# Attention and a mixture of experts on one core: zero stores put in another order around the weights, one weight load issued earlier in the queues, the last scaling split over two engines

## The chip, the core and the metric

The kernel runs on one core of a Trainium2 chip. The core has a matrix engine (TensorE, PE in the profile, with its weight loads as PEld), a vector engine (VectorE, DVE), a scalar engine (ScalarE, ACT), a general engine (GpSimd, POOL) and a queue engine (SyncE, SP) that issues transfers. Sixteen transfer engines move data between the core's memory and HBM. The metric is the device time of one execution in microseconds; lower is better.

## The reference, cut to what matters

The first part is attention inside chunks of 64 positions, for 8 batches, 8 heads and 576 positions of 64 numbers. Its output, seen as 4608 tokens of 512 numbers, goes into a layer of 8 experts. Each token goes to the expert with the largest logit; of these an expert keeps at most 80, those with the largest gate. All other rows of the output are zero.

```
logits = x @ w_gate
expert_idx = np.argmax(logits, axis=1)
...
out = np.zeros((N, D), dtype=np.float32)
for e in range(E):
    ...
    if len(tok_idx) > capacity:
        gw = gate_w[tok_idx]
        keep = np.argpartition(-gw, capacity)[:capacity]
        tok_idx = tok_idx[keep]
    h = np.maximum(x[tok_idx] @ w1[e], 0.0)
    out[tok_idx] = gate_w[tok_idx, None] * (h @ w2[e])
```

Each expert has 2 MiB of first-layer weights (512 x 1024, float32) and 2 MiB of second-layer weights (1024 x 512). The output has 9 MiB.

## The kernel before, in words

Three stages follow each other. In the first, to about 127 us, the attention is computed and its result x stored in HBM (`xs`), and the gates are counted on the way. In the second, to about 142 us, the kept tokens of each expert are found and numbered; TensorE runs matmuls without use (`keep_warm`) between the short steps. The third stage is the experts'.

There the kept tokens stand in 768 slots, 96 to an expert, in six rounds of 128 slots (r = 0 to 5), four groups of 32 slots each, so that a round takes in two or three experts. Rounds 0 and 1 use experts 0 to 2, round 2 experts 2 and 3, round 3 experts 4 and 5, round 4 experts 5 and 6, round 5 experts 6 and 7. `experts` writes out the order of one round:

- `gather(r)`: an indirect load from `xs` on POOL's queue. Rounds 0 to 2 are gathered whole (tile `xg`) at the start of the stage, rounds 3 to 5 in four quarters each (`quarters`, tile `xq`), paced by a copy of one column on POOL.
- `xpose(r)`: transposes on TensorE and copies on ScalarE (`xt`).
- `layer1(r, 0)` and `layer1(r, 1)`: the first layer for two groups each, L237; ReLU on ScalarE (`hs`), a transpose on VectorE (`ht`).
- `layer2(r)`, called one round later: the second layer, L254, its sum `y` scaled by the gates on VectorE into `ys` (L259).
- `scatter(r)`: an indirect store of the 128 scaled rows into `out` on POOL's queue. The scatters of rounds 0, 1 and 2 are written out together after round 3, the others one by one.

All weights and all zero stores go through SP's queue, in the order in which they are written out. The weights are issued a part at a time by `part(e, l)`: expert e, layer l (0 or 1); w1_3 below is part(3, 0), the fourth expert's first-layer weights, and w2_6 is part(6, 1). Experts 0 and 1 are loaded during the attention, experts 2, 3, 4 and 7 share three buffers, and 5 and 6 take those of 0 and 1. `clear(n)` stores zeros over 512 rows of `out` (1 MiB), `clear(3.5, nc.sync, 2)` over 256. A scatter waits until all of them have landed.

A part can be held back: `part(..., after)` first copies one column of `after` into the new tile, and the load has to wait for that copy. Before, w1_3 is held back by `si`, the scatters' row numbers, which VectorE ends with. `ahead(r, xg)` is called as `extra` after the first gathers and after each round: with r = 0 it issues w1_4 and w2_3, held back until the second gather has landed; r = 1 issues w1_5, w2_4 and the zero stores `CLEARS[1]`; r = 2 issues w1_6, w2_5 and `CLEARS[2]`; r = 3 issues w1_7 and w2_6; r = 4 issues w2_7.

So SP's queue before, from 122 us on, holds: w2_2, zeros 0, zeros 2, w1_3, zeros 3.5, w1_4, w2_3, w1_5, w2_4, zeros 1, 4, 5, w1_6, w2_5, zeros 6, 7, 8, w1_7, w2_6, w2_7.

A block for the general case stands behind the experts (L1179); its condition is false with these inputs.

Of the kernel before, what the change touches and what calls it, by code (L numbers as in the profile page):

```python
# [11 lines left out]
AF = mybir.ActivationFunctionType  # L12
ALU = mybir.AluOpType
# [13 lines left out]
DM = 512  # L27
FF = 1024
SL = 96
NR = NE * SL // P  # L30
# [3 lines left out]
NWARM = 17  # L34
WARM = (2, 3, 5)
BIG = 8192.0
CLEARS = {1: (1, 4, 5), 2: (6, 7, 8)}
NQ = 3
ON_POOL = (0, 1)
STEPS_AFTER = 6  # L40
# [29 lines left out]
def attention_moe(ctx: ExitStack, tc: tile.TileContext, qk0, qv, kh, wg, w1, w2, cap, cst, out):  # L70
    nc = tc.nc
# [22 lines left out]
    scale = cp.tile([40, NE], F32, name="scale")  # L94
# [94 lines left out]
    def experts(pool, pp, gi, si, gate, getw, tag, extra=None, quarter=None):  # L189
        groups = [[(4 * r + g) // 3 for g in range(4)] for r in range(NR)]  # L190
        xg, xT, hT, hs, ys_ = {}, {}, {}, {}, {}

        def gather(r):
            t = pool.tile([P, DM], F32, name=f"xg{tag}{r}", tag="xg", bufs=NQ if extra else 2)
            nc.gpsimd.indirect_dma_start(
                out=t, out_offset=None, in_=xs[:, :],
                in_offset=bass.IndirectOffsetOnAxis(ap=gi(r), axis=0),
                bounds_check=NT * 512 - 1, oob_is_err=False)
            xg[r] = t

        def xpose(r):
            t = pool.tile([P, 4, P], F32, name=f"xt{tag}{r}", tag="xt")
            n = 4 if r else 2
            for b0 in range(0, 4, n):
                pm = pp.tile([P, n, P], F32, name=f"xp{tag}{r}_{b0}", tag="hp" if b0 else "xp",
                             bufs=2 if b0 else 1)
                for b in range(n):
                    nc.tensor.transpose(
                        pm[:, b, :], xg[r].rearrange("p (m b) -> p b m", b=4)[:, b0 + b], ident)
                nc.scalar.copy(t[:, b0:b0 + n], pm)  # L210
            xT[r] = t.rearrange("p b (g t) -> p g b t", g=4)

        def quarters(r, after):
            pace = pool.tile([P, 1], F32, name=f"pace{tag}{r}", tag="pace", bufs=1)
            nc.gpsimd.tensor_copy(pace, after)
            t = pool.tile([P, DM], F32, name=f"xq{tag}{r}", tag="xg", bufs=NQ)
            for g in range(4):
                nc.gpsimd.indirect_dma_start(
                    out=t[:, P * g:P * g + P], out_offset=None,
                    in_=xs.rearrange("r (c d) -> (r c) d", c=4),  # L220
                    in_offset=bass.IndirectOffsetOnAxis(ap=quarter(4 * r + g), axis=0),
                    bounds_check=NT * 2048 - 1, oob_is_err=False)
            xg[r] = t

        def xpose_blocks(r):
            t = pool.tile([P, 4, 4, 32], F32, name=f"xt{tag}{r}", tag="xt")
            nc.vector.transpose(t, xg[r].rearrange("p (g t b) -> p g b t", g=4, b=4))
            xT[r] = t

        def layer1(r, f):  # L230
            h = pp.tile([P, 2, 256], F32, name=f"h{tag}{r}_{f}", tag="h", bufs=4)
            for j in range(2):
                g = 2 * f + j
                w = getw(groups[r][g])[0]
                for b in range(4):
                    for c in range(4):
                        nc.tensor.matmul(  # L237
                            h[32 * c:32 * c + 32, j, :], lhsT=xT[r][:, g, b, :],
                            rhs=w[:, b, 256 * c:256 * c + 256],
                            start=(b == 0), stop=(b == 3), tile_position=(0, 32 * c))  # L240
            a = pool.tile([P, 512], F32, name=f"hs{tag}{r}_{f}", tag="hs", bufs=1)
            nc.scalar.activation(a, h.rearrange("p j n -> p (j n)"), AF.Relu)  # L242
            t = pool.tile([P, 2, 8, 32], F32, name=f"ht{tag}{r}_{f}", tag=f"ht{f}")
            nc.vector.transpose(t.rearrange("p j b n -> p (j b n)"), a)  # L244
            hs[r] = a[:, 0:1]
            hT[r, f] = t

        def layer2(r):
            y = (pp.tile([P, DM], F32, name=f"y{tag}{r}", tag="h", bufs=4) if extra and r == NR - 1
                 else pp.tile([P, DM], F32, name=f"y{tag}{r}", tag="y", bufs=1))  # L250
            for c in range(8):
                for g in range(4):
                    o = 32 * g
                    nc.tensor.matmul(  # L254
                        y[o:o + 32, :], lhsT=hT[r, g // 2][:, g % 2, c, :],
                        rhs=getw(groups[r][g])[1][:, c, :],
                        start=(c == 0), stop=(c == 7), tile_position=(0, o))
            ys = pool.tile([P, DM], F32, name=f"ys{tag}{r}", tag="ys", bufs=3 if extra else 1)
            nc.vector.tensor_scalar(ys, y, gate[:, r:r + 1], None, op0=ALU.mult)  # L259
            ys_[r] = ys  # L260

        def scatter(r):
            nc.gpsimd.indirect_dma_start(  # L263
                out=out, out_offset=bass.IndirectOffsetOnAxis(ap=si[:, r:r + 1], axis=0),
                in_=ys_.pop(r), in_offset=None, bounds_check=NT * 512 - 1, oob_is_err=False)

        for r in range(NQ if extra else 2):
            gather(r)
        if extra:
            extra(0, xg)  # L270
        xpose(0)
        for r in range(NR + 1):
            if r < NR:
                layer1(r, 0)
            if r + 1 < (NQ if extra else NR):
                xpose(r + 1)
            if r < NR:
                layer1(r, 1)
            if extra and NQ <= r + 1 < NR:
                xpose_blocks(r + 1)  # L280
            if extra and NQ <= r + 2 < NR:
                quarters(r + 2, hs[r])
            if not extra and r + 2 < NR:
                gather(r + 2)
            if r >= 1:
                layer2(r - 1)
            if extra:
                extra(r + 1, xg)
            while ys_ and (r >= NQ or not extra):
                scatter(min(ys_))  # L290


    with ExitStack() as actx:
# [539 lines left out]
        def clear(n, eng=nc.scalar, m=4):  # L833

            r0 = int(512 * n)
            eng.dma_start(
                out[r0:r0 + P * m].rearrange("(p c b) d -> p c (b d)", p=P, b=2),
                zero[:, None, :].to_broadcast([P, m // 2, 2 * DM]))
# [38 lines left out]
        with tc.manual_schedule():  # L877
# [234 lines left out]
            gate, sv = targets(mp, [(pl0, gi0), (pl1, gi1)], "c")  # L1112
# [19 lines left out]
            si = mp.tile([P, NR], I32, name="si")  # L1132
# [11 lines left out]
    with tc.manual_schedule():  # L1144
        with ExitStack() as ectx:
            ep = ectx.enter_context(tc.tile_pool(name="exp", bufs=2, reuse_waits="tile"))
            pp = ectx.enter_context(tc.tile_pool(name="pexp", bufs=2, space=PSUM,
                                                 reuse_waits="tile"))

            def part(e, l, after=None):  # L1150

                w = weights.setdefault(e, [None, None])
                pool = wp if e in (5, 6) else wp2
                a, n = ((4, FF), (8, DM))[l]
                w[l] = pool.tile([P, a, n], F32, name=f"w{l + 1}_{e}", tag=f"w{l + 1}")
                if after is not None:
                    nc.vector.tensor_copy(w[l][:, 0, 0:1], after)
                fetch(w[l], e, l, 0, a)

            def ahead(r, xg):  # L1160

                if r < 5:
                    for e, l in (((4, 0), (3, 1)), ((5, 0), (4, 1)),
                                 ((6, 0), (5, 1)), ((7, 0), (6, 1)), ((7, 1),))[r]:
                        part(e, l, xg[1][:, 0:1] if r == 0 else None)
                for n in CLEARS.get(r, ()):
                    clear(n, nc.sync)

            part(2, 0)
            part(2, 1)  # L1170
            clear(0, nc.sync)
            clear(2, nc.sync)
            part(3, 0, si[:, 0:1])
            clear(3.5, nc.sync, 2)
            experts(ep, pp, lambda r: gi1[:, r - 1:r] if r else gi0, si, gate, weights.get, "c",
                    ahead, lambda g: giq[:, g % 4, g // 4 - NQ:g // 4 - NQ + 1])


    with tc.If(nc.values_load(flag_i[0:1, 0:1], min_val=0, max_val=1) > 0):  # L1179
        with ExitStack() as gctx:  # L1180
# [9 lines left out]
            with ExitStack() as lctx:  # L1190
                lp = lctx.enter_context(tc.tile_pool(name="gpl", bufs=1, space=PSUM))
                with tc.For_i(0, 28, 1):
# [10 lines left out]
                        th, pc, capt, th, op0=ALU.is_ge, op1=ALU.mult)  # L1203
# [36 lines left out]
            with tc.For_i(0, nc.values_load(nr[0:1, 0:1], min_val=0, max_val=48), 1):  # L1240
                with ExitStack() as lctx:
                    xp = lctx.enter_context(tc.tile_pool(name="gx", bufs=1))
                    si = xp.tile([P, NR], I32, name="gsi")
                    with ExitStack() as pctx:
# [4 lines left out]
                        gate, sv = targets(xp, [pl], "g")  # L1249
# [90 lines left out]
```

## Time and profile before

| | us |
|---|---|
| median of three runs | 240.34 |
| the three runs | 239.62, 240.34, 243.28 |
| profiled execution | 239.95 |
| its span, first to last instruction | 238.2 |
| TensorE busy | 220.3 |
| VectorE busy | 130.5 |
| ScalarE busy | 73.7 |
| POOL busy | 64.2 |

The profile is of one execution. A row of the timeline gives the start in us from the span's beginning, the length, the engine, the line, the operation and its tiles (written<-read, buffer numbers left out, a tile's name often with a `c` at its end), and in brackets the idle time before it and what ended that. A row of an operation's table gives the shortest, median and longest time in ns, and the first and last start. A row by stretch has for each engine its busy time and, in parentheses, its number of instructions (PE, PEld, DVE, ACT, POOL), then TensorE's granted clock as a share of the full one, the share of time in which the transfer engines were busy, and what they moved in GB/s. "SPq" and "POOLq" are what the queues of these engines do themselves, such as issuing a transfer.

### The profile page before, as it was taken

The page shows a single profiled execution, that of the slowest core. Times are in us where ns is not written, and L with a number is a line of the kernel's source. Part 1 is how long each engine was busy: PE and PEld are TensorE (multiplying, and loading weights), DVE is VectorE, ACT ScalarE, POOL GpSimd, SP SyncE. Part 2 cuts the span into 40 slices and gives each one's busy share as a digit, 9 for nine tenths or more (in the row PEclk, how much of TensorE's full clock was granted, in tenths as well). Part 3 has the DMA queues.
Part 4 walks back from the last instruction along what each step waited for, and adds up shares of the span by engine and source line. Part 5 has one row for each costly group of instructions (what it writes and reads, how often), then busy time and mean ns, then how long its engine had stood idle before and what let it go on. Part 6 is the DMA issues. An engine that isn't in the chain of part 4 may idle for free. (4 is left out here: it accounts for less than half of the span.)

```text
span 238.2 us, 8194 instructions
## 1 busy us (share of the span) xinstructions
PE 220.3 (92%) x3513; PEld 140.8 (59%) x3513; DVE 130.5 (55%) x411; ACT 73.7 (31%) x161; POOL 64.2 (27%) x145
## 2 busy tenths in 40 slices
PE   7998999998998999999998999999999999999910
PEld 5787787876787787878764635643535344453300
DVE  6587697878689898969877771121122214020110
ACT  3124434342645445666764411210101101020000
POOL 9001221121203047473534050015070420111130
PEclk9999999999999999999999999999999999999995
DMA  6999999999999999999999939999999999994120
GB/s 214 358 408 389 408 415 407 416 410 417 410 415 409 389 413 382 405 349 388 375 406 416 416 128 316 376 415 400 398 417 414 411 412 418 411 412 158 66 76 1
DMA packets 24121, 84.81 MB, mean 356 GB/s; under 512 B 2768, under 2 KB 2896, under 8 KB 24080
## 3 DMA queue, kind: packets, MB, share of 16 engines
q1 hardware_dynamic: 20272, 71.84, 76.4%
q0 software_dynamic: 3664, 12.32, 13.4%
q8 instruction: 30, 0.49, 0.8%
q10 hardware_dynamic: 144, 0.07, 0.2%
q14 instruction: 11, 0.09, 0.1%
HBM read 64.03 MB, written 20.45 MB: 355 GB/s over the span
## 5 line engine op out<-in xcount | busy, mean ns | idle before, releaser
L237 PE MATMUL hc<-w,xtc 128*32 128x256 f32 x768 | 42.8, 379 | 0.2 <-ACT xtc L210 0.2
L254 PE MATMUL yc<-w,htc 128*32 128x512 f32 x384 | 42.1, 592 | 0.0
L401 PE MATMUL s<-kz,qv 128*64 128x128 f32 x544 | 37.2, 279 | 0.0
L237 PEld LDWEIGHTS hc<-w,xtc 128*32 128x32 f32 x768 | 24.7, 110 | 18.3 <-issue 2.4
L437 ACT ACTIVATE pT<-pt 128x512 f32<-128x512 f32 x36 | 21.4, 594 | 37.0 <-PE pt L435 36.9
L401 PEld LDWEIGHTS s<-kz,qv 128*64 128x64 f32 x544 | 29.0, 136 | 5.7 <-issue 5.6
L417 DVE TENSOR_REDUCE mx<-s 128x8 f32<-128x512 f32 (+1 forms) x37 | 24.9, 674 | 12.6 <-PE s L401 12.3
L254 PEld LDWEIGHTS yc<-w,htc 128*32 128x32 f32 x384 | 12.5, 110 | 26.6 <-issue 25.7
L460 PEld LDWEIGHTS o<-qv,pT 64*64 64x64 f32 x1120 | 19.9, 134 | 12.0 <-issue 8.2
L242 ACT ACTIVATE hsc<-hc 128x512 f32<-128x512 f32 x12 | 7.2, 597 | 62.7 <-PE hc L237 62.7
L244 DVE STREAM_TRANSPOSE htc<-hsc 128x512 f32<-128x512 f32 x12 | 8.5, 710 | 32.9 <-ACT hsc L242 32.9
L460 PE MATMUL o<-qv,pT 64*64 64x65 f32 x1120 | 25.0, 224 | 1.1 <-issue 0.8
L419 DVE TENSOR_TENSOR sm<-s,mx 128x512 f32<-128x512 f32 (+1 forms) x37 | 24.7, 667 | 0.1
L479 DVE TENSOR_TENSOR x<-o,rc 128x512 f32<-128x512 f32 x35 | 24.1, 689 | 0.8
L435 PE MATMUL pt<-ct,sm 128*128 128x128 f32 x144 | 23.9, 289 | 0.0
L259 DVE TENSOR_SCALAR ysc<-yc,gatec 128x512 f32<-128x512 f32 x6 | 4.5, 751 | 34.3 <-PE yc L254 26.2
L497 PE MATMUL px<-ct,x 128*128 128x128 f32 x136 | 20.5, 273 | 0.0
L498 ACT COPY xT<-px 128x512 f32<-128x512 f32 x32 | 18.6, 580 | 0.0
L575 POOL TENSOR_TENSOR comp<-comp,ct 128x32 bf16<-128x32 bf16 x18 | 3.9, 237 | 50.2 <-DVE rc L474 40.6
L435 PEld LDWEIGHTS pt<-ct,sm 128*128 128x128 f32 x144 | 15.6, 143 | 2.4
L497 PEld LDWEIGHTS px<-ct,x 128*128 128x128 f32 x136 | 15.9, 140 | 0.8 <-issue 0.8
L263 POOL DMA_INDIRECT out<-ysc,si x6 | 6.0, 994 | 32.6 <-issue 12.6
(205 smaller groups left out, 231.5 us busy)
## 6 DMA issues: line engine op xcount, KB each, us to landing
w<-in_w SPq DMA_DIRECT2D x12, 2048.0 KB, 21.6
qv<-in_qv SPq DMA_DIRECT2D x14, 1032.0 KB, 11.4
kz<-in_kh SPq DMA_DIRECT2D x34, 256.0 KB, 10.4
xs<-x POOLq DMA_DIRECT2D x8, 1024.0 KB, 10.5
w<-in_w SPq DMA_DIRECT2D x8, 1024.0 KB, 11.2
out<-zero SPq DMA_DIRECT2D x8, 1024.0 KB, 19.4
qv<-in_qv SPq DMA_DIRECT2D x2, 520.0 KB, 8.9
qv<-in_qv SPq DMA_DIRECT2D x2, 516.0 KB, 9.4
```

The source lines that it names most:

```text
L237: nc.tensor.matmul(h[32 * c:32 * c + 32, j, :], lhsT=xT[r][:, g, b, :], rhs=w[:, b, 256 * c:256 * c + 256], start=(b == 0), stop=(b == 3), ...
L244: nc.vector.transpose(t.rearrange("p j b n -> p (j b n)"), a)
L254: nc.tensor.matmul(y[o:o + 32, :], lhsT=hT[r, g // 2][:, g % 2, c, :], rhs=getw(groups[r][g])[1][:, c, :], start=(c == 0), stop=(c == 7), ...
L401: nc.tensor.matmul(o, lhsT=a, rhs=b, start=True, stop=True)
L417: nc.vector.tensor_reduce(m8, s8, axis=AX.X, op=ALU.max)
L419: d['sub'] = lambda: nc.vector.tensor_tensor(d8, s8, to, op=ALU.subtract)
L435: nc.tensor.transpose(pt[:, pr, :], sv[:, pr, :], ident)
L437: nc.scalar.activation(pT, pt, AF.Exp, scale=0.125)
L460: nc.tensor.matmul(po[h][64 * u:64 * u + 64, 65 * pr:65 * pr + 65], lhsT=d['pT'][64 * h:64 * h + 64, pr, 64 * u:64 * u + 64], rhs=TT[T, r] ...
L479: nc.vector.tensor_tensor(x8, pov[..., 0:64], to, op=ALU.mult)
L497: nc.tensor.transpose(pm[:, pr, :], t['x'][:, r, P * pr:P * pr + P], ident)
L498: copy(t['xT'][:, :, P * r:P * r + P], pm)
```

## The change

Three things change.

1. The zero stores' order. Zeros 2 no longer stand ahead of the experts; they are stored in `CLEARS[2]`, and zeros 6 move from there into `CLEARS[1]`.
2. w1_3 and the half store behind it (zeros 3.5) are issued from a call of `ahead` with r = -1 that stands between the second and the third gather. What holds w1_3 back is now a copy of a gate column on POOL's queue, which stands behind the second gather's issue, in place of the copy of `si` on VectorE.
3. The last round's scaling is done in two halves of 256 columns, the first on VectorE, the second on ScalarE as a copy with a scale.

SP's queue then holds: w2_2, zeros 0, w1_3, zeros 3.5, w1_4, w2_3, w1_5, w2_4, zeros 1, 4, 5, 6, w1_6, w2_5, zeros 2, 7, 8, w1_7, w2_6, w2_7.

```
-CLEARS = {1: (1, 4, 5), 2: (6, 7, 8)}
+CLEARS = {1: (1, 4, 5, 6), 2: (2, 7, 8)}
...
-            nc.vector.tensor_scalar(ys, y, gate[:, r:r + 1], None, op0=ALU.mult)
+            h = DM // 2 if extra and r == NR - 1 else DM
+            nc.vector.tensor_scalar(ys[:, 0:h], y[:, 0:h], gate[:, r:r + 1], None, op0=ALU.mult)
+            if h < DM:
+                nc.scalar.activation(ys[:, h:], y[:, h:], AF.Copy, scale=gate[:, r:r + 1])
             ys_[r] = ys
...
         for r in range(NQ if extra else 2):
             gather(r)
+            if extra and r == 1:
+                extra(-1, gate)
         if extra:
             extra(0, xg)
...
-            def part(e, l, after=None):
+            def part(e, l, after=None, eng=nc.vector):
...
                 if after is not None:
-                    nc.vector.tensor_copy(w[l][:, 0, 0:1], after)
+                    eng.tensor_copy(w[l][:, 0, 0:1], after)
                 fetch(w[l], e, l, 0, a)
 
             def ahead(r, xg):
 
+                if r < 0:
+                    part(3, 0, xg[:, 0:1], nc.gpsimd)
+                    clear(3.5, nc.sync, 2)
+                    return
...
             clear(0, nc.sync)
-            clear(2, nc.sync)
-            part(3, 0, si[:, 0:1])
-            clear(3.5, nc.sync, 2)
             experts(ep, pp, lambda r: gi1[:, r - 1:r] if r else gi0, si, gate, weights.get, "c",
                     ahead, lambda g: giq[:, g % 4, g // 4 - NQ:g // 4 - NQ + 1])
```

## The prediction

> **What bounds the kernel now.** I read the page's two top sections, then the chain that ended last, then the timeline of the expert part from 137 us on, and last single landings of transfers.
>
> ```profile
> PE 220.3 (92%) x3513; PEld 140.8 (59%) x3513; DVE 130.5 (55%) x411; ACT 73.7 (31%) x161; POOL 64.2 (27%) x145
> ...
> 226.43 0.98 DMA out<-ysc,si
> ...
> 230.19 0.69 POOL out L263
> ```
>
> TensorE is busy nearly all the time, but the chain at the end is not its own: it goes from scatter to scatter on the POOL queue. The timeline of the end shows why.
>
> ```profile
> 203.01 1.02 POOL L263 DMA_INDIRECT out<-ysc,si  x1 [10.66 <-SPq L1179]
> 206.30 7.09 PE L237 MATMUL hc<-w,xtc 128*32 128x256 f32 x128
> 210.88 1.01 POOL L263 DMA_INDIRECT out<-ysc,si  x1 [6.85 <-DMA out<-ysc,si]
> 213.21 13.92 PE L254 MATMUL yc<-w,htc 128*32 128x512 f32 x128
> 218.55 0.98 POOL L263 DMA_INDIRECT out<-ysc,si  x1 [6.66 <-issue]
> 221.98 0.98 POOL L263 DMA_INDIRECT out<-ysc,si  x1 [2.45 <-DVE ysc L259]
> 226.43 0.98 POOL L263 DMA_INDIRECT out<-ysc,si  x1 [3.47 <-issue]
> 227.19 0.75 DVE L259 TENSOR_SCALAR ysc<-yc,gatec 128x512 f32<-128x512 f32 x1 [6.12 <-PE yc L254]
> 229.90 0.98 POOL L263 DMA_INDIRECT out<-ysc,si  x1 [2.49 <-issue]
> ```
>
> The six scatters write one tensor and go one at a time. Scatter 4 leaves at 226.43 although its matmuls (the first half of the 13.92 us) ended near 220.2; scatter 5 leaves at 229.90 although its scaling ended at 227.94. What starts this chain is the last zero store. The next fence has, for single transfers, the issuing instruction (its start is the last time but one in the row) and under it the time to landing: the last zero store (rows 4096 to 4607) and scatter 0. The two rows at its end are SP's notices of landed weights: that of w1_7 (first layer of expert 7), and six whose first is w2_6 and whose last is w2_7 (second layers).
>
> ```profile
> L836 SPq DMA_DIRECT2D out<-zero x1: 2448/2448/2448, 182.7 to 182.7; - x1
> DMA to landing us min/median/max: 19.4/19.4/19.4
> ...
> L263 POOL DMA_INDIRECT out<-ysc,si x1: 1025/1025/1025, 203.0 to 203.0; - x1
> DMA to landing us min/median/max: 7.0/7.0/7.0
> ...
> L1179 SPq EVENT_SEMAPHORE  x1: 17/17/17, 207.1 to 207.1; - x1
> ...
> L1179 SPq EVENT_SEMAPHORE  x6: 17/17/17, 212.5 to 218.4; - x6
> ```
>
> The last zeros land at 182.7 + 19.4 = 202.1, scatter 0 leaves 0.9 us later, lands at 210.0 behind the weights; scatter 2 follows scatter 1 as late (7.7 us), and from 218.55 on the spacings are 3.43, 4.45 and 3.47 us. The weights are close behind too: w2_6 lands at 212.5 and is wanted at 213.2 by the second layer, w1_7 lands at 207.1 and is wanted by the second group of layer 1, a quarter of 7.09 us after 206.30, at 208.1. w2_7 lands by 218.4 and is wanted at 220.2. So three streams end almost together: TensorE with 0.7 to 2 us to spare, the weights, and the scatters, which are last.
>
> All of it hangs on one transfer queue. The page's row of 40 slices has its engines at nine tenths or more but for the first slice, one at 137 to 143 us and those from 214 on:
>
> ```profile
> DMA  6999999999999999999999939999999999994120
> ...
> 138.00:139.00 1.00, 1.00 (x17) 0.27 (x15) 1.00 (x10) 0.00 (x0) 0.36 (x1) 1.00 0.08 33
> 140.00:141.00 1.00, 1.00 (x8) 0.39 (x6) 0.90 (x7) 0.00 (x0) 0.95 (x1) 1.00 0.15 57
> 155.00:160.00 5.00, 5.00 (x84) 2.48 (x77) 1.14 (x2) 0.93 (x2) 0.36 (x2) 1.00 1.04 421
> 165.00:170.00 5.00, 5.00 (x100) 3.03 (x96) 1.39 (x2) 0.60 (x1) 0.00 (x0) 1.00 1.03 393
> ```
>
> In the rows by stretch the last two columns are the share and the rate (GB/s) of the transfer engines. Soon after 137 us they have little to do.
>
> **The change, part by part.** Times here are against the profiled execution (239.95 us, span 238.2), which lies 0.4 us under the median of the three runs.
>
> *The zero stores.* Store 2 and its landing, as above for single transfers:
>
> ```profile
> L836 SPq DMA_DIRECT2D out<-zero x1: 641/641/641, 123.7 to 123.7; - x1
> DMA to landing us min/median/max: 17.3/17.3/17.3
> ```
>
> Before, stores 0 and 2 (1 MiB each) go out one behind the other from 123 us on, the second landing at 123.7 + 17.3 = 141.0, and fill most of the queue until about 137. After, store 2 leaves that place and goes into the later round; store 6 moves up a round, ahead of w1_6 and w2_5. So the full queue gets 1 MiB more, all of it ahead of the last zero store and of w1_7, w2_6 and w2_7, and the idle stretch grows by as much. At 421 and 393 GB/s 1.049 MB take 2.49 and 2.67 us: I take 2.55 (some 411 GB/s). The Trainium skill ("DMA: Bandwidth & Descriptors", Specifications) gives about 358 GB/s as the limit of memory traffic for one core. By it the store would cost an estimated 2.9 us and the sum below would be some +2.3; the rows, at 393 and 421, stand against it.
>
> What the removal frees is the first gather.
>
> ```profile
> 137.21 1.15 POOL L195 DMA_INDIRECT xgc<-xs,gic  x1 [2.93 <-DVE bt L1077]
> 139.94 1.00 POOL L195 DMA_INDIRECT xgc<-xs,gic  x1 [1.58 <-DVE rowc L182]
> 140.32 1.10 PE L828 MATMUL pwarm<-ct 128*128 128x512 f32 x2
> 141.25 1.00 POOL L195 DMA_INDIRECT xgc<-xs,gic  x1 [0.30 <-issue]
> 141.66 0.75 PE L208 MATMUL xpc<-ct,xgc 128*128 128x128 f32 x4 [0.24 <-DMA xgc<-xs,gic]
> 141.88 0.15 DVE L1157 CAST w<-si 128x1 f32<-128x1 int32 x1
> 142.06 0.38 SPq L113 DMA_DIRECT2D w<-in_w  x1
> 144.16 0.15 DVE L1157 COPY w<-xgc 128x1 f32<-128x1 f32 x1 [1.94 <-DMA xgc<-xs,gic]
> ...
> 153.95 0.75 PE L208 MATMUL xpc<-ct,xgc 128*128 128x128 f32 x4
> ...
> 172.87 0.18 POOL L215 COPY pacec<-hsc 128x1 f32<-128x1 f32 x1 [8.11 <-ACT hsc L242]
> 173.67 1.02 POOL L218 DMA_INDIRECT xqc<-xs,giq  x1 [0.62 <-DVE htc L244]
> ```
>
> Its transposes wait 0.24 us for it, since the warm-keeping matmuls hold TensorE until 141.42. However early it lands, the experts begin at most 0.24 us sooner, and that only lengthens the wait for weights: nothing at the end.
>
> *w1_3 behind the second gather.* The pacing copy moves from VectorE (141.88) to POOL, between gather 1 (ends 140.94) and gather 2. Like the copy at 172.87 it takes 0.18, and the next gather follows 0.62 later, so gather 2 leaves some 0.7 us later, near 142.0. Gather 1 took 4.2 us from its start to 144.16; gather 2, beside the weights, may take more, but its transposes stand at 153.95 (the last xpc row): free. The copy starts between 140.95 and 141.25, as gather 2 did; its source, the gates, is long done. SP can issue w1_3 between 141.2 and 141.5 instead of 142.06, 0.6 us earlier, and the half store behind it as well. That is the gain: the stream starts 0.6 us sooner (bounds 0.3, should POOL take the copy up late, and 0.85). SP then waits for gather 1 as before (144.16): 2.5 MiB are queued, over 6 us of work, so the queue does not run dry even if gather 1, now beside w1_3, lands 1 us later. VectorE is rid of 0.15 us that nobody waits for.
>
> *The last scaling in halves.*
>
> ```profile
> L259 DVE TENSOR_SCALAR ysc<-yc,gatec 128x512 f32<-128x512 f32 x6 | 4.5, 751 | 34.3 <-PE yc L254 26.2 <-DMA out<-ysc,si 8.1
> L210 ACT COPY xtc<-xpc 128x256 f32<-128x256 f32 x2 | 0.6, 375 | 2.3 <-PE xpc L208 2.3
> ```
>
> 751 becomes about 400 ns, with ScalarE's half beside it at 375: 0.35 us earlier, at most 0.38, at worst 0 (if ScalarE is as slow as VectorE's whole). It is hidden behind scatter 4's landing, by 229.90 - 227.94 = 2.0 us. Without that cover it would be worth its 0.35.
>
> *The sum.* Stream: +2.55 - 0.6 = +1.95 (bounds +1.6 and +2.4). Then w1_7 lands at 209.05, where the second group of layer 1 could go on at 207.85: a stall of 1.2 us; w2_6 at 214.45 against 214.15, 0.3 more; w2_7 at 220.35 is wanted only at 221.4. TensorE ends at 214.45 + 13.92 = 228.4, against 227.13. The last zeros land at 204.05; scatter 0 leaves near 204.95, lands near 212.0, and as the weights behind it are as many as before, the whole chain keeps its distances: scatter 5 leaves at 231.85, with y scaled at 228.8. The end of the kernel follows scatter 5 as now. So +1.95 us: 241.9 from the profiled execution, 242.3 from the median. I say 242.0: the profiled execution lies between the two lower of the three runs (239.62 and 240.34), and stands for a usual one.
>
> The chain has a play of its own: from scatter 3 to 4 it took 4.45 us where its neighbours took 3.43 and 3.47. I leave that as it is, but 1 us may go, or come at another scatter. With the stream's bounds that makes +0.6 to +3.4, or 240.6 to 243.4.
>
> **Rivals.** *Not slower: the queue's slowest engine decides, and it loses nothing.* After 138 us the transfer rate is down to 33 and 57 GB/s: a few of the 16 engines lag. Store 2 lands only at 141.0, against w1_3's issue at 142.06. If the engine that lags sets the later landings too and its lag lasts into w1_3, it never pauses: its transfers are as many as before in either order, store 2's place costs it nothing, and what is left is the 0.6 us of w1_3: scatter 5 at 229.3, 239.4 us. It decides once the lag reaches past w1_3's issue, 1.1 us more than it does. Against it: 141.0 lies before 142.06, so the lag is gone when the stream starts. 0.16.
>
> *Slower, by a second long landing.* ScalarE's last instructions, now over long before, move behind its half of the scaling, beside scatter 5. If that, or the shifted weights, gives two more spacings of 4.45 instead of 3.45 us, the chain has +1.95 + 2 = 243.9. For it: of the three late spacings one is that long. Against: no weights are in flight there. 0.11.
>
> *A long hold-up, and the clock with it.*
>
> ```profile
> 227.00:228.00 1.00, 0.12 (x4) 0.00 (x0) 0.75 (x1) 0.00 (x0) 0.41 (x1) 1.00 0.05 20
> ...
> 232.00:233.00 1.00, 0.00 (x0) 0.00 (x0) 0.00 (x0) 0.00 (x0) 0.00 (x0) 0.54 0.07 29
> ```
>
> The second row is the first stretch of 1 us in which the granted clock (0.54) is not full, some 5 us after the last matmul (0.12 us into the row of 227); the expected stall is 1.2. So the clock needs a stall four times as long, such as POOL's copy would make if it were held up: 3.5 us there bring the stream, and with it the end, 3.5 us later still, to 245.4, even at full clock. 0.04.
>
> *It does not do what it says*: w1_3 may go no earlier, if POOL's copy starts after gather 2's old time. That is +2.55, inside the forecast's bounds.
>
> **Chances and range.** Forecast 0.69, not slower 0.16, long landings 0.11, stall or hold-up 0.04. The range takes the forecast's bounds and reaches to the not-slower case's 239.4 and the long landings' 243.9. Two per cent (4.8 us) is about what a measurement of this kernel can tell from no change: faster than 235.5 no case gives (0.02 for what I overlooked), slower than 245.1 the last one, 0.05; within, 0.93.
>
> **What would show it.** Right: w1_3 issued near 141.4; the transfer queue idle from about 134.5; the last zero store landing near 204; PE waiting for a weight transfer at L237 and L254 near 208 and 214; scatters 0 and 5 near 205 and 231.9; scatter 5 still released by scatter 4 and not by the scaling. Wrong: zeros landing at 202 or before, no wait for weights, or scatter 5 released by the halves. The prediction fails as a whole if the stream is not full, so that 1 MiB more finds room.

## The result and the profile after

The changed kernel takes 242.44 us (median of 22 runs, 240.31 to 244.5), the kernel before 239.44 (22 runs, 238.62 to 243.28). The ratio, from undisturbed runs, is 1.0104, 95% interval 1.0079 to 1.0129: slower by 1.0%, some 2.5 us (3.0 by the two medians). The forecast was +2.0 us, 242.0 in all.

The profile shown is of an execution of 240.31 us, the quickest of the 22, so the 2.5 us are not all in it. Its span is 238.2 us, as before. First its page's rows by 40 slices (transfer share and rate), then the stretches of 1 us with engines, clock, share and rate:

```profile
DMA  6999999999999999999999649999999999996220
GB/s 220 354 406 389 410 415 407 415 413 416 410 415 411 390 407 396 404 338 396 379 406 414 266 107 334 409 411 398 402 418 414 411 407 411 413 415 259 74 73 8
...
134.00:135.00 1.00, 0.95 (x12) 0.64 (x11) 0.18 (x1) 0.17 (x1) 0.05 (x1) 1.00 0.61 246
...
137.00:138.00 1.00, 1.00 (x4) 0.44 (x3) 1.00 (x8) 0.00 (x0) 1.00 (x1) 1.00 0.00 0
```

The queue empties in the slice from 131 us on (266 GB/s) and moves nothing from 137 to 138. Before, it was full until 137:

```profile
134.00:137.00 3.00, 2.94 (x28) 2.13 (x27) 1.63 (x11) 0.22 (x2) 0.19 (x1) 1.00 1.01 414
```

The idle stretch has grown by the 1 MiB taken out of it. The start of the experts, from the timeline of the changed kernel:

```profile
136.99 1.15 POOL L195 DMA_INDIRECT xgc<-xs,gic  x1 [2.93 <-DVE bt L1082]
139.72 1.01 POOL L195 DMA_INDIRECT xgc<-xs,gic  x1 [1.58 <-DVE rowc L182]
140.72 0.21 POOL L1162 COPY w<-gatec 128x1 f32<-128x1 f32 x1
140.95 0.37 SPq L113 DMA_DIRECT2D w<-in_w  x1
141.03 0.64 PE L208 MATMUL xpc<-ct,xgc 128*128 128x128 f32 x4
141.08 1.02 POOL L195 DMA_INDIRECT xgc<-xs,gic  x1 [0.16 <-issue]
```

POOL's copy stands right behind the second gather and w1_3 leaves at 140.95, 3.96 us after the first gather where it was 4.85: 0.89 us sooner. This execution reached the experts 0.22 us earlier than that of before, so distances from the first gather say more than the times themselves.

The end: SP's notices of landed transfers, then the timeline.

```profile
L1185 SPq EVENT_SEMAPHORE  x2: 17/17/17, 201.9 to 203.4; - x2
L1185 SPq EVENT_SEMAPHORE  x1: 17/17/17, 208.5 to 208.5; - x1
L1185 SPq EVENT_SEMAPHORE  x6: 17/17/17, 214.3 to 220.7; - x6
...
204.33 1.02 POOL L266 DMA_INDIRECT out<-ysc,si  x1 [12.73 <-SPq L1185]
208.53 5.39 PE L237 MATMUL hc<-w,xtc 128*32 128x256 f32 x96 [1.07 <-SPq L1185]
213.74 14.50 PE L254 MATMUL yc<-w,htc 128*32 128x512 f32 x128
222.87 0.98 POOL L266 DMA_INDIRECT out<-ysc,si  x1 [2.44 <-DVE ysc L260]
226.76 0.98 POOL L266 DMA_INDIRECT out<-ysc,si  x1 [2.91 <-issue]
228.28 0.48 DVE L260 TENSOR_SCALAR ysc<-yc,gatec 128x256 f32<-128x256 f32 x1 [6.12 <-PE yc L254]
228.80 0.47 ACT L262 ACTIVATE ysc<-yc,gatec 128x256 f32<-128x256 f32 x1 [14.22 <-DVE ysc L260]
230.25 0.98 POOL L266 DMA_INDIRECT out<-ysc,si  x1 [2.51 <-ACTq L1185]
```

The last zeros land at 203.4 (202.1 before), w1_7 at 208.5 (207.1), w2_6 at 214.3 (212.5). TensorE, which did not wait for weights before, stands still for 1.07 us ahead of 208.53. The bracket names SP's own notice, as that comes at the moment w1_7 lands. The last row of L254 is 14.50 us long instead of 13.92, and w2_6, which its third group needs at once, lands 0.6 us after the row's start. Scatter 0 leaves 67.34 us after the first gather (65.80 before), scatter 5 93.26 (92.69).

### The profile page after: what moved, and what is told of

Its sections match the earlier page's. It is cut to its first block, busy times and chain, and to the rows that moved or that the text cites. A ratio compares the mean times of both kernels' runs of the same rounds, so it can differ in the third digit from the quotient of the medians.

```text
span 238.2 us, 8197 instructions
## 1 busy us (share of the span) xinstructions
PE 218.9 (92%) x3513; PEld 142.3 (60%) x3513; DVE 130.0 (55%) x410; ACT 74.2 (31%) x162; POOL 64.8 (27%) x146
## 5 line engine op out<-in xcount | busy, mean ns | idle before, releaser
L254 PE MATMUL yc<-w,htc 128*32 128x512 f32 x384 | 42.7, 592 | 0.0
L254 PEld LDWEIGHTS yc<-w,htc 128*32 128x32 f32 x384 | 15.7, 110 | 24.0 <-issue 17.1
L260 DVE TENSOR_SCALAR ysc<-yc,gatec 128x512 f32<-128x512 f32 (+1 forms) x6 | 4.2, 706 | 36.3 <-PE yc L254 26.8
```

Source lines behind the costliest of these rows:

```text
L254: nc.tensor.matmul(y[o:o + 32, :], lhsT=hT[r, g // 2][:, g % 2, c, :], rhs=getw(groups[r][g])[1][:, c, :], start=(c == 0), stop=(c == 7), ...
```

## The experiments

All ran beside the kernel before, and times are against it. In the expectations, "stream theory" is the prediction's account: the transfer queue is full, so that bytes put into it delay everything behind them. Each profile is of one execution.

**The three parts, each alone, and the changed kernel again.**

`e1_zeros_only`:

```
-CLEARS = {1: (1, 4, 5), 2: (6, 7, 8)}
+CLEARS = {1: (1, 4, 5, 6), 2: (2, 7, 8)}
...
-            clear(2, nc.sync)
```

> Only the zero stores' order is changed (store 2 late, store 6 a round earlier); the fourth expert's first weights and the last scaling are as before. Stream theory (1 MiB more behind 142 us, all of it ahead of the last zeros and the last weights, at some 410 GB/s): +2.5 us against the kernel before, at least +1.5; last zeros land near 204.6 instead of 202.1, TensorE waits for w1_7 by about 1.3 us more than before. Rival, the halves: the loss comes from the last scaling, whose second half began only after the first one (0.48 and 0.47 us); then this kernel is within 0.5 us of before. Rival, the lagging engine: the place of store 2 costs nothing; within 0.5 us of before, last zeros near 202.1.

Measured: ratio 1.0105 (1.0059 to 1.0152), 242.25 against 239.94 us. The zero stores alone give the whole of the loss, within the intervals. From its timeline, w1_3's issue, scatter 0, the wait for w1_7 and scatter 5:

```profile
141.93 0.37 SPq L113 DMA_DIRECT2D w<-in_w  x1
...
205.27 1.02 POOL L263 DMA_INDIRECT out<-ysc,si  x1 [13.46 <-SPq L1178]
209.45 5.39 PE L237 MATMUL hc<-w,xtc 128*32 128x256 f32 x96 [1.45 <-SPq L1178]
231.95 0.98 POOL L263 DMA_INDIRECT out<-ysc,si  x1 [2.60 <-issue]
```

Scatter 0 leaves 63.34 us after w1_3's issue; before it was 203.01 - 142.06 = 60.95. One MiB is 2.4 us. Scatter 5 leaves 2.05 us later than before, the profiled time is 241.87 against 239.95.

`e2_early_w_only` has the changed kernel's `ahead(-1)` and POOL's copy, and the zeros and the scaling of before.

> Only the fourth expert's first weights (and the half store behind them) are issued earlier, behind the second gather by way of POOL; zeros and scaling as before. Stream theory: the stream starts 0.6 to 0.9 us sooner, nothing is added: -0.4 to -0.9 us against before; last zeros land near 201.3, scatter 5 leaves that much sooner, until the scaled rows (about 228.7) bound it. Rival, the gathers suffer from weights that are let in earlier: +0.3 us or more, by a first gather that lands later.

Measured: ratio 0.9995 (0.9968 to 1.0021). The interval allows a gain of 0.8 us, and shows none.

```profile
137.39 1.15 POOL L195 DMA_INDIRECT xgc<-xs,gic  x1 [2.93 <-DVE bt L1079]
...
141.35 0.38 SPq L113 DMA_DIRECT2D w<-in_w  x1
...
202.28 1.03 POOL L263 DMA_INDIRECT out<-ysc,si  x1 [10.28 <-DVE xtc L227]
229.32 0.98 POOL L263 DMA_INDIRECT out<-ysc,si  x1 [2.80 <-DMA out<-ysc,si]
```

In the profile the gain is there: w1_3 3.96 us behind the first gather, scatter 0 64.89 behind it (65.80 before), scatter 5 91.93 (92.69). But this execution came to the first gather 0.18 us later, so 0.6 us are left at scatter 5. The landing of scatter 5 then took 3.9 us (3.0 before), and the execution came out at 240.26 us against 239.95: nothing of the gain is left at this execution's end.

`e3_halves_only` has only the last scaling in halves.

> Only the last scaling is split in halves over two engines. Stream theory: hidden behind scatter 4's landing, 0 us, within 0.4 us of before; scatter 5 still leaves near 229.9. Rival, the halves: as they run one behind the other they end near 228.2 + 0.1 and cost a semaphore more, and ScalarE's end of program comes later: +1 us or more.

Measured: ratio 0.9995 (0.9965 to 1.0026). The halves cost nothing, as expected here; but they do not run beside each other, as the prediction had it:

```profile
226.42 0.48 DVE L260 TENSOR_SCALAR ysc<-yc,gatec 128x256 f32<-128x256 f32 x1 [6.12 <-PE yc L254]
226.94 0.47 ACT L262 ACTIVATE ysc<-yc,gatec 128x256 f32<-128x256 f32 x1 [13.66 <-DVE ysc L260]
...
229.15 0.98 POOL L266 DMA_INDIRECT out<-ysc,si  x1 [2.49 <-issue]
```

ScalarE waits for VectorE. Together they take 0.99 us, longer than the whole scaling's 0.75, and scatter 5 leaves 1.7 us later anyway.

`e4_changed_again`, without an edit:

> The changed kernel once more, beside its parts. Stream theory: +2 to +3 us against before, and the sum of the three parts within 0.7 us. Its first profile came from an execution of 240.31 us, the quickest of 22; a usual one should show the last zeros landing later than the 203.4 of that one, near 204 to 205, and scatter 5 leaving near 232.

Measured: ratio 1.0113 (1.0057 to 1.0168), 242.85 us; the parts give +2.2 by medians, the whole +2.9. The 0.7 us between them are less than the interval of either side (over 1 us each way), so that the edits cost more together than apart is neither shown nor excluded. Its profiled execution was again a quick one (241.08 us), with scatter 0 at 204.39 and scatter 5 at 230.50. So the usual execution of 242.4 us was not seen, and the expectation of scatter 5 near 232 stays untested.

**Without store 2.** Both kernels leave rows 1024 to 1535 unzeroed.

`e5_changed_no_store2`:

```
-CLEARS = {1: (1, 4, 5, 6), 2: (2, 7, 8)}
+CLEARS = {1: (1, 4, 5, 6), 2: (7, 8)}
```

> The changed kernel without zero store 2: rows 1024 to 1535 of the output are not zeroed. Stream theory: 1 MiB less in the full queue, 2.5 us less than the changed kernel, that is 0 to -0.9 us against before; last zeros near 201.2, no wait of TensorE for w1_7. Rival, the halves: no difference from the changed kernel beyond 0.7 us.

Measured: ratio 1.0049 (1.0024 to 1.0073), +1.0 us by medians. Taking the 1 MiB out of the full queue gives back over half of the loss, not all: less than expected. In its profile w1_3 leaves at 141.57 and scatter 0 at 203.74, 62.17 us later, where the other kernels with as many bytes took 60.6 to 61.3; and TensorE still waits 0.68 us for w1_7, where no wait was expected.

`e6_before_no_store2` takes `clear(2, nc.sync)` out of the kernel before.

> The kernel before without zero store 2: rows 1024 to 1535 of the output are not zeroed. Stream theory: the store at 123 us cost nothing, as it fell into an idle stretch of the queue: within 0.5 us of before; the idle stretch begins 2.5 us sooner and the experts start at most 0.24 us sooner. Rival, the lagging engine or a first gather held up by the store: 0.7 us or more faster, with the last zeros landing that much sooner.

Measured: ratio 0.9989 (0.9962 to 1.0015). At its old place the store costs nothing that the times show. The stretches before the experts show that it filled idle time (with the store, the first of them stood at 1.01 and 414 GB/s, as above):

```profile
134.00:137.00 3.00, 2.94 (x25) 1.95 (x25) 1.97 (x14) 0.19 (x1) 0.13 (x1) 1.00 0.21 83
137.00:140.00 3.00, 2.94 (x34) 1.14 (x32) 2.58 (x21) 0.17 (x1) 1.41 (x2) 1.00 0.28 87
```

Its scatter 0 leaves 60.82 us after w1_3's issue (141.72 and 202.54), the same as before, so no engine's lag was carried into the stream.

**More zeros ahead of the experts.** `e7_early_w_half_ahead` is `e2_early_w_only` with the half store in the idle stretch:

```
             clear(0, nc.sync)
             clear(2, nc.sync)
+            clear(3.5, nc.sync, 2)
...
                 if r < 0:
                     part(3, 0, xg[:, 0:1], nc.gpsimd)
-                    clear(3.5, nc.sync, 2)
                     return
```

> Zeros 0 and 2 at their old places and the half store 3.5 moved there too, into the idle stretch; the fourth expert's first weights issued early by POOL; scaling as before. Stream theory: 0.5 MiB less in the full queue (1.3 us) and 0.6 to 0.9 us sooner: the last zeros land near 200, the scatters come about 1.9 us sooner, and then the scaled rows bound scatter 5 (near 228.7 instead of 229.9): -1.2 us against before, at most -2. Rival, the first gather is held up by the half store, which pushes the store's lag to 142 us: experts start 1 us later, 0 to +1 us against before.

Measured: ratio 0.9965 (0.9942 to 0.9989), 238.88 against 239.55 us: faster than both kernels; its profiled execution took 238.74 us, 1.2 less than that of before.

```profile
141.42 0.75 PE L208 MATMUL xpc<-ct,xgc 128*128 128x128 f32 x4
...
200.23 1.02 POOL L263 DMA_INDIRECT out<-ysc,si  x1 [8.14 <-SPq L1183]
212.95 13.92 PE L254 MATMUL yc<-w,htc 128*32 128x512 f32 x128
226.94 0.75 DVE L259 TENSOR_SCALAR ysc<-yc,gatec 128x512 f32<-128x512 f32 x1 [6.12 <-PE yc L254]
227.97 0.98 POOL L263 DMA_INDIRECT out<-ysc,si  x1 [4.53 <-DVE ysc L259]
```

Scatter 0 leaves 2.8 us sooner than before, and the chain of scatters is no longer last. Scatter 5 now waits for the scaling (4.53 <-DVE ysc), 1.9 us sooner than before; its landing took 3.7 us instead of 3.0. TensorE never waits for weights. The gain of 0.7 to 0.8 us is less than the 1.2 expected.

`e8_two_stores_ahead` puts store 1 there as well.

> As the kernel just before this one, with zero store 1 moved ahead of the experts as well. Stream theory alone: 1 MiB less in the full queue, but no more than the scaled rows allow, -1.2 us against before. Against that the zeros now last to about 141 us and the first gather (issued at 137.2) has to share the queue with them: like the quarter gathers in the full queue it takes 5.7 us and more instead of 4.4, the experts start 1.3 us later or more, and TensorE, now bound by nothing else, ends as much later: 0 to +2 us.

Measured: ratio 1.0094 (1.0053 to 1.0134).

```profile
140.00:141.00 1.00, 1.00 (x9) 0.57 (x8) 0.83 (x8) 0.16 (x1) 0.64 (x1) 1.00 1.02 418
...
137.63 1.15 POOL L195 DMA_INDIRECT xgc<-xs,gic  x1 [2.92 <-DVE bt L1079]
...
144.32 0.75 PE L208 MATMUL xpc<-ct,xgc 128*128 128x128 f32 x4 [2.48 <-DMA xgc<-xs,gic]
...
217.55 13.92 PE L254 MATMUL yc<-w,htc 128*32 128x512 f32 x128
232.56 0.98 POOL L263 DMA_INDIRECT out<-ysc,si  x1 [5.88 <-DVE ysc L259]
```

Now the queue is full while the first gather runs. The gather's rows are used 6.7 us after its issue, where the other kernels took 4.04 to 4.45, TensorE waits 2.48 us, and all that follows it is late. The wait costs more than its length: behind it TensorE's granted clock fell to 0.50. The next two rows are this kernel's, the last is the same group of matmuls before.

```profile
145.00:150.00 5.00, 4.78 (x57) 2.55 (x60) 0.31 (x2) 0.51 (x2) 0.00 (x0) 0.66 1.02 407
145.29 5.35 PE L237 MATMUL hc<-w,xtc 128*32 128x256 f32 x64 [0.22 <-ACT xtc L210]
...
142.63 3.66 PE L237 MATMUL hc<-w,xtc 128*32 128x256 f32 x64 [0.22 <-ACT xtc L210]
```

At a mean clock of 0.66 the first 64 matmuls took 1.7 us longer. That closes the account against the kernel just above: the first transposes start 2.9 us later (144.32 and 141.42), the last row of L254 4.6 us later (217.55 and 212.95). Behind w2_2 there is room for 2.5 MiB of zeros and not for 3.5.

**Does the order count beside the bytes?** This was asked because of the run without store 2. `e9_store6_earlier` changes `CLEARS` to `{1: (1, 4, 5, 6), 2: (7, 8)}` and leaves store 2 ahead of the experts.

> The kernel before with nothing but zero store 6 a round earlier, ahead of w1_6 and w2_5 (zeros 0 and 2 stay ahead of the experts). Stream theory by bytes alone: as many bytes as before ahead of the last zeros, w1_7, w2_6 and w2_7: 0 us, within 0.5 us of before; last zeros some 60.0 us after w1_3's issue. Rival, the order of the transfers counts beside their bytes (the changed kernel without store 2 was 1.2 us slower than before although it holds no more bytes behind 142 us): +0.7 to +1.3 us, last zeros 61 us and more after w1_3's issue.

Measured: ratio 1.0017 (0.9995 to 1.0039), 239.45 against 239.55 us by medians. SP's notice of the last zeros is at 201.7, 60.4 us after w1_3's issue (141.29), and scatter 0 leaves 61.30 us after it (202.59). Both are nearer to the bytes alone than to the rival's 61 us and more for the zeros. The interval reaches to 0.9 us, so the times by themselves do not exclude the rival's +0.7; they show no cost of the order.

`e10_store2_late_6_in_place` takes store 2 out ahead and sets `CLEARS` to `{1: (1, 4, 5), 2: (2, 6, 7, 8)}`.

> The kernel before with nothing but zero store 2 moved behind w2_5 (ahead of store 6, which stays in its round). Stream theory by bytes: +2.5 us as with both moved, last zeros 62.5 us after w1_3's issue. Rival, the order counts: with store 6 in place +1.2 to +1.8 us.

Measured: ratio 1.0135 (1.0102 to 1.0167): the bytes cost as much with store 6 in its place, here rather more (3.2 us). So it is store 2's move into the full queue that costs, and not store 6's. The profiled execution took 244.62 us, the longest of the six, with scatter 0 64.25 us after w1_3's issue (142.51 and 206.76), and shows what a slow end looks like. The first row has POOL's queue waiting twice, from 225.3 ahead of scatter 4 and from 228.7 ahead of scatter 5, with the shortest, middle and longest wait in ns; the second row is scatter 4.

```profile
L263 POOLq EVENT_SEMAPHORE  x2: 2859/4021/5183, 225.3 to 228.7; - x2
L263 POOL DMA_INDIRECT out<-ysc,si x1: 985/985/985, 228.9 to 228.9; - x1
...
210.94 7.07 PE L237 MATMUL hc<-w,xtc 128*32 128x256 f32 x96 [2.81 <-SPq L1178]
211.00:215.00 4.00, 4.00 (x44) 2.09 (x48) 0.75 (x1) 0.49 (x1) 1.01 (x1) 0.57 1.02 412
231.82 0.75 DVE L259 TENSOR_SCALAR ysc<-yc,gatec 128x512 f32<-128x512 f32 x1 [6.12 <-PE yc L254]
234.62 0.98 POOL L263 DMA_INDIRECT out<-ysc,si  x1 [4.78 <-issue]
```

The wait for w1_7 has grown to 2.81 us, and here too the granted clock fell behind it, to a mean of 0.57 over 4 us: the 96 matmuls took 7.07 us, where they took 5.39 in `e1_zeros_only`. Ahead of scatter 5 POOL waited 5.18 us, ahead of scatter 4 2.86. The scaling ended at 232.57, scatter 5 left 2.05 us after that; in the quicker kernel above it was 0.28. So this end is slow for two reasons: 1.7 us by the clock, and some 1.8 us by one late release in the chain of scatters. What held that release is not shown; the profile has no landing of scatter 4.

**The halves.** `e11_scaling_beside`: VectorE scales the whole as before, and ScalarE scales the second half once more into a tile of its own that nobody reads.

```
+            if extra and r == NR - 1:
+                other = pool.tile([P, DM // 2], F32, name="other", tag="other", bufs=1)
+                nc.scalar.activation(other, y[:, DM // 2:], AF.Copy, scale=gate[:, r:r + 1])
```

> The kernel before; ScalarE besides scales the second half of the last round once more, into a tile of its own that nobody reads, so that the two engines share only the sum in PSUM. If the halves ran one behind the other because they write one tile, ScalarE starts here with VectorE, within 0.2 us of 227.2. If it is the reading of one PSUM sum that keeps them apart, ScalarE starts when VectorE's 0.75 us are over. The time stays within 0.8 us of before either way.

Measured: 239.66 us, one run.

```profile
227.10 0.75 DVE L259 TENSOR_SCALAR ysc<-yc,gatec 128x512 f32<-128x512 f32 x1 [6.01 <-PE yc L254]
227.89 0.47 ACT L262 ACTIVATE other<-yc,gatec 128x256 f32<-128x256 f32 x1 [13.92 <-DVE ysc L259]
```

With an output tile of its own ScalarE still starts only when VectorE has ended, at 227.85. So the common output tile is not the reason. What the two still share is the sum in PSUM, TensorE's output memory, which both only read, and it is a semaphore from VectorE that ScalarE waits for. The kernel before has the same thing elsewhere: L1069 and L1071 read one sum of TensorE's and write tiles of their own, and ScalarE starts when VectorE has ended, at 135.01.

```profile
134.83 0.18 DVE L1069 TENSOR_REDUCE kc<-s 128x8 f32<-128x24 f32 x1 [0.87 <-PE s L1057]
135.05 0.19 ACT L1071 CAST cb<-s 128x40 bf16<-128x40 f32 x1 [1.02 <-DVE kc L1069]
```

Of the tile `sh`, which VectorE writes and which does not lie in PSUM, the same two engines read side by side (starts at 122.33 and 122.34). This fits the shared sum as the reason; no run here gives each engine a sum of its own, so it is not proved.

`e12_early_w_half_ahead_halves` is `e7_early_w_half_ahead` with the halves.

> The kernel with the early weights and the half store ahead of the experts (0.8 us faster than before), with the last scaling in halves. There scatter 5 waited for the scaling itself, 0.75 us, so the cover is gone. If the halves run one behind the other (0.48, 0.05 and 0.47 us), scatter 5 leaves 0.2 to 0.3 us later than in that kernel: -0.6 us against before. If they ran beside each other it would leave 0.3 us sooner: -1.1 us. The timing may not tell these apart; the timeline does, by scatter 5's start behind the end of L254 (1.0 us with the whole scaling).

Measured: ratio 0.9987 (0.9961 to 1.0014). L254 ends at 212.62 + 14.04 = 226.66 and scatter 5 leaves at 227.97, 1.31 us behind it; with the whole scaling it was 1.10 (226.87 and 227.97). Where the cover is gone the halves cost 0.2 us, by the timeline of one execution each.

## Why the prediction was right, step by step

- **The 1 MiB and its price: right.** Forecast 2.55 us. From w1_3's issue to scatter 0 the kernel before took 60.95 us, the zeros alone 63.34, the changed kernel 204.33 - 140.95 = 63.38: 2.4 us. By the 358 GB/s of the Trainium skill ("DMA: Bandwidth & Descriptors", Specifications) it would be an estimated 2.9 us; the measured 2.4 stand against it.
- **That store 2 cost nothing at its old place: right**, by the run without it (0.9989). The lagging-engine rival falls with the same run, and with the zeros alone, which it had at no change.
- **w1_3 sooner: right in sign, a term sized too small.** 0.89 us and not 0.6; POOL took up its copy at once (140.72), and the next gather followed 0.16 us after it, where 0.62 was taken from the pacing copies. So the stream was only 1.5 us late in the profile (67.34 against 65.80), not 1.95. In the timed runs this part gives nothing that can be told from 0, and the loss of the changed kernel is that of the zeros alone (1.0104 and 1.0105). That would account for the forecast of +1.95 lying below both.
- **The waits of TensorE: right.** 1.07 us for w1_7 (1.2 forecast); the 0.58 by which the last L254 row is longer stand where 0.3 was forecast for w2_6.
- **The first gather: what the removal was said to free is not seen.** At most 0.24 us was forecast. From the first gather to the transposes it is 4.04 us now and was 4.45, but with store 2 at its old place it is 4.04 as well in `e2_early_w_only` (137.39 and 141.43) and in `e9_store6_earlier` (136.44 and 140.48). So the 0.4 us are not the store's. The weights bound the end of TensorE's work all the same.
- **The clock: wrong.** The prediction took the 5 us from the last matmul to the first stretch with less than the full clock for the length of a wait that lowers it. Waits of 2.48 us (`e8_two_stores_ahead`) and 2.81 us (`e10_store2_late_6_in_place`) were enough, and cost 1.7 us each on top. The waits of 1.07 us here and 1.45 us in `e1_zeros_only` left the clock at 1.00, so the forecast did not suffer; but the margin was about 1 us, and not the factor of four.
- **The halves beside each other: wrong.** They run one behind the other, 0.99 us in all; the gain of 0.35 us does not exist. The cover hid the mistake, as it would have hidden the gain.
- **Scatter 5 bound by scatter 4: right**, in the profile at 230.25 with the scaling over at 229.27. The bracket of that row names ScalarE's queue; but where the scaling does bind (`e7_early_w_half_ahead`) the scatter leaves 0.28 us behind it and not 0.98, and POOL's idle time of 2.51 us is that of before (2.49).
- **The whole chain keeping its distances: not in this execution.** From scatter 0 to scatter 5 it took 25.92 us instead of 26.89: scatter 0 landed in 6.4 us instead of 7.0, scatter 3 in 3.1 instead of 3.7. So scatter 5 was only 0.35 us later, where the runs have +2.5. In the profile of `e1_zeros_only` the chain took 26.68 us, and there scatter 5 is 2.05 us later.

Open: the changed kernel's runs are spread over 4 us with no gap, those of before, but for two, over 2.2. The forecast's second long landing would do it, and the kernel with store 2 late and store 6 in place shows a wait of 5.18 us for one release and a fall of the clock, but no usual execution of the changed kernel itself was profiled. Its mean clock does not sort its runs (0.978 at 241.93 us, 0.984 at 243.7). Nor is it explained why the changed kernel without store 2 stays 1.0 us slower than before: neither the early weights, nor the halves, nor the missing store, nor store 6's place makes a measurable difference alone.

## What to carry to other kernels

Find out what the queue does at the place that a transfer leaves, not only at the place where it goes: taken out of an idle stretch and put into a full one, 1 MiB of zeros cost its whole 2.4 us, and half a MiB moved the other way, with the early weights, gave 0.8. An idle stretch ahead of a latency-bound load has a capacity; 2.5 MiB of stores fitted here, 3.5 MiB made the load over 2 us later. Look at the clock behind a wait of TensorE's before putting a price on the wait: 2.5 us cost 1.7 more here. Look at what the end waits for before splitting work over engines, and whether they then take turns, as these two did at one sum.

## What had not been expected of the hardware

With no weights in flight any more, the wait between two scatters of 128 rows took 2.9 us at one time and 5.2 at another. TensorE's granted clock was halved behind waits of 2.48 and 2.81 us, and was not behind 1.07 and 1.45. Behind the last matmul the first stretch of 1 us below the full clock began after 5 us before and after 2 us in the changed kernel, so the time is not a fixed one.

Whether a half store in the stream costs more than its bytes stays open. From w1_3's issue to scatter 0 it took 60.93 us with it (202.28 - 141.35) and 59.20 without (200.23 - 141.03), 1.7 us for 0.52 MB, which at 410 GB/s would be 1.3; but kernels with the same bytes differ by more than these 0.4 us.
